# Six of layer 0's normalisations on GpSimd instead of VectorE, with new orders for the front

## The chip, the cores and the metric

The kernel runs on one core of one Trainium2 chip. The core has five engines that run side by side, each working through its own list of instructions in order: TensorE (PE in the profile; its weight loads are PEld), VectorE (DVE), ScalarE (ACT), GpSimd (POOL) and SyncE (SP), which here only starts DMAs. They wait for one another on semaphores. The metric is the device time of one execution in microseconds (us).

## The reference

A block of four layers works on x, 2048 tokens of 448 features, in bfloat16.

```
x = x + A(layernorm(x));  x = x + B(layernorm(x))     # layers 0 and 1
x = x + A(layernorm(x));  x = x + B(layernorm(x))     # layers 2 and 3

layernorm(x) = (x - mean) / sqrt(var + 1e-5)           # over the 448 features, no weights
A: qkv = x @ wqkv; 16 heads of 28; each token attends to 8 tokens,
   itself and those 2, 4, ... 14 before it; softmax; @ wo
B: (x @ w_gate) * (x @ w_up) @ w_down                  # 448 -> 1792 -> 448
```

## The kernel before

**Tiling.** Tokens lie on partitions in 16 blocks of 128 (even tokens first, then odd ones, so that a stride of 2 becomes a neighbour). Layer 0 projects its queries and keys in five chunks of 256, 512, 512, 512 and 256 tokens: chunk 0 is blocks 0 and 1, chunk 1 blocks 2 to 5, chunk 2 blocks 6 to 9, chunk 3 blocks 10 to 13, chunk 4 blocks 14 and 15. The attention works in groups of 120-token query tiles (group 0 has one, the others two).

**A block's way in layer 0** (`ln_chunk`): a DMA loads it into `x_sb`; VectorE takes its statistics (L584, `bn`) and combines them (L586, `mv`); ScalarE makes the inverse deviation with a logarithm and an exponential (L587, L589, `rstd`), for one, two or four blocks at a time; one instruction normalises (L605, `xn`), reading 2 x 256 features of `x_sb` (the two stretches overlap, so that 448 features become four rows of 128) and writing 512 bfloat16 values to one of five slots of `xn_sb`, block B to slot B modulo 5; TensorE transposes them into PSUM (L615, L619, `Tps`); ScalarE or VectorE evicts the transposed block into `xnTa` (L626, L629, `T`). Before, all sixteen `xn` of layer 0 are VectorE's.

**What follows.** TensorE projects queries and keys (`xnTa` with `WQK`) and values (`xnTa` with `WV`), both at L353. ScalarE or VectorE evicts them (L715 for queries and keys, L780 to L807 for values). VectorE masks the queries for two heads (L826, `Qz`), TensorE makes the scores (L838, `Sh`), ScalarE their exponentials (L848, `Ex`), VectorE the minimum with a mask `MK` (L855), TensorE the weighted values (L873, `Ah`); their copies and sums (L887, L891), the normalisation by the denominators (L901 to L914) and the output projection (`wo_g`, L353) end the layer. `WQK` is filled from a staging buffer by eight copies (L523, `wqk`), which the first projection waits for, and eight small ones (L531, `wqp`), which those from chunk 2 on wait for.

**What sets the order.** Nothing is decided on the chip. `build` creates the operations (`sc.add`) and numbers them as they come; each names the engines that may run it, its dependencies and a planned duration. `ORDER` holds, written out for each engine, the numbers in the order in which the engine runs them; an operation runs on the engine in whose list its number stands. `BANKS` gives each user of PSUM its banks of eight; an operation that takes a bank waits for the instruction that evicts the bank's last holder. `emit` turns all of it into instructions with semaphore waits. A wait stops the engine's whole list. TensorE starts with sixteen matmuls on a cleared buffer (`warm`, L515), among which the transposes of blocks 0 and 1 stand.

The planned durations (325.0 for an `xn`) are used by no instruction. `HEAD_P`, priorities and planned durations have no effect on the program once the orders are written out.

Of the kernel before, what the change touches and what calls it, by code (L numbers as in the profile page):

```python
# [5 lines left out]
ALU = mybir.AluOpType  # L6
# [91 lines left out]
def grp_nc(g):  # L98
# [36 lines left out]
    ),  # L135
    "dve": (
# [18 lines left out]
    ),  # L155
    "pool": (
        "24 18 28 29 25 39 40 32 33 35 41 26 20 22 21 30 27 36 19 31 34 42 37 43 44 68 66 38 77 23 76"
    ),
# [223 lines left out]
def build(nc, A_x, A_wqkv, A_wo, B_w_gate, B_w_up, B_w_down, out):  # L382
# [16 lines left out]
    mv = sb([128, NBLK, 2], dt.float32, "mv")  # L399
    lnv = sb([128, NBLK], dt.float32, "lnv")  # L400
    rstd = sb([128, NBLK], dt.float32, "rstd")
# [26 lines left out]
    sc = Sched()  # L428
# [9 lines left out]
    def one(fn, key=None):  # L438
        return [(fn, key)]
# [134 lines left out]
    def ln_chunk(li, j, prio):  # L574
        par = li % 2
# [552 lines left out]
```

## Time and profile before

| what | value |
|---|---|
| median of 3 runs | 380.56 us (380.43 to 381.18) |
| the profiled execution, its own time | 380.47 us |
| its span, first to last instruction | 378.7 us |
| TensorE busy | 373.6 us |
| VectorE busy | 285.4 us |
| ScalarE busy | 200.0 us |
| GpSimd busy | 7.8 us |
| granted TensorE clock, mean | 1.0 |

Times inside the execution count from the span's start. A busy TensorE is not one at its peak: the ends of its pipelined matmuls are modelled, and consecutive ones overlap in the rows, so its pace is read from start to start. A row of the timeline gives start, length, engine, line, operation, what it writes and reads, the shapes and the number of instructions merged; in brackets the engine's idle time before it and what ended it. A row of a group gives the number of instructions, then busy time in all and the mean of one in ns, then idle time before them. GpSimd's copies and mask building fill the first 11 us; after 22 us it does nothing.

### The profile page before, as it was taken

What the parts mean: (1) busy time and instruction counts of PE and PEld (TensorE: products, weight loads), DVE (VectorE), ACT (ScalarE), POOL (GpSimd) and SP (SyncE); (2) the same over time, 40 slices, a digit from 0 to 9 for tenths busy, and PEclk for the clock granted to TensorE, in tenths of its full rate; (3) what the DMA queues carried; (4) which work ended last, traced back from release to release, by engine and by line L of the source; (5) the groups of instructions that cost most, each with busy time, mean ns of one, the idle gap of its engine ahead of it and who ended that gap; (6) DMA issues with size and microseconds to landing.
All of it is one profiled execution on the core that took longest, in us unless ns stands there. A gap on an engine that the chain in (4) does not pass through costs nothing.

```text
span 378.7 us, 14371 instructions
## 1 busy us (share of the span) xinstructions
PE 373.6 (99%) x6376; PEld 208.7 (55%) x6376; DVE 285.4 (75%) x647; ACT 200.0 (53%) x384; POOL 7.8 (2%) x35
## 2 busy tenths in 40 slices
PE   8999999999999999999999999999999999999997
PEld 3645577644554445544676666645555444445764
DVE  7998999999867953878698598559699778446324
ACT  4897895778715355246548215638647533043310
POOL 6000000000000000000000000000000000000000
PEclk9999999999999999999999999999999999999999
DMA  7665544500250216312104123510106102312002
GB/s 260 167 163 144 112 113 95 81 10 13 31 86 5 58 28 93 43 28 50 25 10 64 27 29 63 93 31 5 29 12 102 35 5 54 74 42 70 2 2 85
DMA packets 56401, 23.10 MB, mean 61 GB/s; under 512 B 46004, under 2 KB 56324, under 8 KB 56340
## 3 DMA queue, kind: packets, MB, share of 16 engines
q1 hardware_dynamic: 56196, 22.14, 28.1%
q8 instruction: 50, 0.82, 0.9%
q14 instruction: 11, 0.09, 0.1%
q10 hardware_dynamic: 144, 0.06, 0.1%
HBM read 8.59 MB, written 2.71 MB: 30 GB/s over the span
## 4 chain that ended last, share of the span: by engine, by line
PE 96%; ACT 2%; POOL 1%; DVE 1%; issue 0%; DVEq 0%; POOLq 0%
PE ps L353 86%; PE ps L356 4%; PE ps L838 2%; PE ps L873 2%; PE ps L997 1%; POOL hT L493 1%; ACT E_sb L848 1%; PE ps L619 0%; PE ps L515 0%; ACT xnTa L626 0%; ACT qk L715 0%; DVE Qz L826 0%; PE ps L615 0%; ACT v_sb L807 0%; ACT xnTa L629 0%
## 5 line engine op out<-in xcount | busy, mean ns | idle before, releaser
L353 PE MATMUL ps<-xnTb,WGU 64*128 64x512 bf16 (+1 forms) x1898 | 173.3, 332 | 0.0
L353 PEld LDWEIGHTS ps<-xnTb,WGU 64*128 64x128 bf16 x1898 | 91.4, 94 | 71.2 <-DVE hT L985 0.6
L982 ACT ACTIVATE g_sb<-ps 128x512 bf16<-128x512 f32 (+1 forms) x140 | 68.9, 509 | 92.4 <-PE ps L353 88.4
L985 DVE TENSOR_TENSOR hT<-g_sb,ps 128x512 bf16<-128x512 bf16 (+1 forms) x140 | 77.4, 573 | 38.2 <-ACT g_sb L982 37.3
L353 PE MATMUL ps<-WD,hT 64*128 64x448 bf16 x786 | 80.8, 349 | 0.0
L353 PEld LDWEIGHTS ps<-WD,hT 64*128 64x128 bf16 x786 | 37.4, 94 | 32.4 <-DVE hT L985 0.2
L353 PE MATMUL ps<-xnTa,WQK 64*128 64x512 bf16 (+1 forms) x490 | 52.1, 352 | 0.0
L946 DVE TENSOR_TENSOR x_sb<-x_sb,ps 128x448 bf16<-128x448 bf16 x62 | 36.6, 611 | 16.4 <-PE ps L353 16.3
L848 ACT ACTIVATE E_sb<-ps,shift_sb 128x1024 bf16<-128x1024 f32 (+1 forms) x36 | 37.9, 1071 | 14.2 <-PE ps L838 13.8
L605 DVE TENSOR_SCALAR xn_sb<-x_sb,mv,rstd 128x896 bf16<-128x896 bf16 (+1 forms) x64 | 35.0, 568 | 6.6 <-ACT rstd L589 5.8
L584 DVE BATCH_NORM_STATS2 st<-x_sb 128x6 f32<-128x448 bf16 x64 | 38.5, 615 | 1.0 <-DMA x_sb<-in_A_x_dram 0.7
L353 PEld LDWEIGHTS ps<-xnTa,WQK 64*128 64x128 bf16 x490 | 23.1, 94 | 20.9 <-DVE WQK L523 0.3
L715 ACT ACTIVATE qk<-ps 128x1024 bf16<-128x1024 f32 (+1 forms) x28 | 25.4, 931 | 14.2 <-PE ps L353 12.0
L902 ACT ACTIVATE R_sb<-R_sb 128x480 f32<-128x480 f32 (+1 forms) x34 | 20.4, 603 | 13.7 <-DVE R_sb L901 13.6
L855 DVE TENSOR_TENSOR E_sb<-E_sb,MK 128x1024 bf16<-128x1024 bf16 (+1 forms) x36 | 23.4, 655 | 4.6 <-ACT E_sb L848 4.6
L914 DVE TENSOR_TENSOR oT<-O_sb,R_sb 128x480 bf16<-128x480 f32 (+5 forms) x38 | 22.2, 600 | 5.3 <-ACT R_sb L903 5.3
L353 PE MATMUL ps<-wo_g,oT 64*128 64x448 bf16 x228 | 25.6, 349 | 0.0
L353 PE MATMUL ps<-WV,xnTa 64*128 64x336 bf16 (+3 forms) x252 | 23.0, 304 | 0.6 <-DVE O_sb L891 0.2
L901 DVE STREAM_SHUFFLE R_sb<-O_sb 128x480 f32<-128x480 f32 (+1 forms) x34 | 23.2, 691 | 0.0
L826 DVE TENSOR_SCALAR Qz<-qk,qmask 128x960 bf16<-128x960 bf16 (+1 forms) x36 | 14.7, 451 | 7.5 <-ACT qk L715 6.5
L903 ACT ACTIVATE R_sb<-R_sb 128x480 f32<-128x480 f32 (+1 forms) x34 | 20.0, 602 | 0.4
L587 ACT ACTIVATE lnv<-mv,eps_sb 128x2 f32<-128x2 f32 (+2 forms) x31 | 8.9, 293 | 19.1 <-DVE mv L586 19.1
(63 smaller groups left out, 221.0 us busy)
## 6 DMA issues: line engine op xcount, KB each, us to landing
out_dram<-x_sb SPq DMA_DIRECT2D x15, 112.0 KB, 1.8
x_sb<-in_A_x_dram SPq DMA_DIRECT2D x3, 448.0 KB, 5.6
hT<-in_A_wqkv_dram SPq DMA_DIRECT2D x4, 224.0 KB, 4.6
WGU<-in_B_w_gate_dram SPq DMA_DIRECT2D x4, 224.0 KB, 3.7
WGU<-in_B_w_up_dram SPq DMA_DIRECT2D x4, 224.0 KB, 4.3
WD<-in_B_w_down_dram SPq DMA_DIRECT2D x2, 448.0 KB, 4.0
WGU<-in_B_w_gate_dram SPq DMA_DIRECT2D x2, 336.0 KB, 4.6
WGU<-in_B_w_up_dram SPq DMA_DIRECT2D x2, 336.0 KB, 4.6
```

The source lines that it names most:

```text
L353: return lambda E: E.matmul(out(), lhs(), rhs(), start=start, stop=stop)
L584: sc.add("dve", one(lambda E, B=B: E.bn_stats(st6[:, B, :], x_sb[:, B, :]), ("bn", li, B)), 525.0, deps=[("x", li - 1, B)] + ([("xn", li - ...
L605: sc.add("dve", one(lambda E, B=B, dst=dst, src=src: E.tensor_scalar(dst, src, mv[:, B, 0:1], rstd[:, B:B + 1], ALU.subtract, ALU.mult), ( ...
L715: return E.activation(dst, src, ACT.Copy) if hasattr(E, "activation") else E.tensor_copy(dst, src)
L848: return E.activation(E_sb[:, slot, 2 * hp:2 * hp + 2, 0:w], ps[:, b0:b0 + 2, 0:w], ACT.Exp, bias=shift_sb[:, 0:1], scale=SCALE)
L855: return E.tensor_tensor(e, e, MK[:, kind, 0:nc].unsqueeze(1).unsqueeze(1).to_broadcast([128, 2, w // nc, nc]), ALU.min)
L901: sc.add("dve", one(lambda E: E.stream_shuffle(R_sb[:, rs, 0:w], O_sb[:, os_, 0:w], [DH] * 32), ("Rs", li, qb)), dve_est(w) + 20.0, deps=[ ...
L902: sc.add("act", one(lambda E: E.activation(R_sb[:, rs, 0:w], R_sb[:, rs, 0:w], ACT.Ln), ("Rl", li, qb)), act_est(w, False), deps=[("Rs", l ...
L914: return E.tensor_tensor(oT[:, :, (a + 256) % HALF:(a + 256) % HALF + z - a], O[:, :, a - tok:z - tok], R_sb[:, rs, 0:w].rearrange("p (h n ...
L946: sc.add("dve", one(lambda E: E.tensor_tensor(x_sb[:, B, :], x_sb[:, B, :], ps[:, bk[w], 0:D], ALU.add), ("x", li, B)), dve_est(D), deps=[ ...
L982: sc.add("act", one(lambda E, gs=gs, bk=bk: E.activation(g_sb[:, gs, 0:nt], ps[:, bk[0], 0:nt], ACT.Copy), ("G", li, j, fc)), act_est(nt), ...
L985: sc.add("dve", one(lambda E, gs=gs, bk=bk, fc=fc: E.tensor_tensor(hT[:, fc, hs, 0:nt], g_sb[:, gs, 0:nt], ps[:, bk[1], 0:nt], ALU.mult), ...
```

## The change

The normalisation of layer 0's blocks from 6 on may now run on GpSimd too, and new lists are written out for all five engines up to about 50 us, with new banks (110 of 299 entries, most of them in the front). The tails of the lists of TensorE (274 of its 404 entries), ScalarE, VectorE and SyncE are unchanged. No operation is added or dropped. Decoded by number, the changes that the prediction speaks of are these.

- GpSimd's list gains `xn` of blocks 8, 7, 12, 11, 10 and 15 (numbers 154, 151, 176, 173, 170, 191); three `wqk` copies (65, 67, 69) and two `wqp` copies (78, 72), and gives one `wqp` copy (76) to VectorE. The identity for the transposes (18, 19) moves to its start, two of the three masks (31, 38) to near its end.
- VectorE's list clears `wo_g` (17) before the warm-up buffer (15), takes block 0 (100, 108) before block 1 (104, 111), and loses the six `xn`, the `wqk` copies 64, 69 and 70, the `T` of blocks 9, 12 and 15 (159, 178, 193) and two key copies of chunk 3 (511, 512). It gains the `T` of blocks 4, 6, 7 and 11 (134, 150, 153, 175), three key copies (202, 362, 598), two value copies (244, 245) and two output copies (220, 256).
- ScalarE's list takes what VectorE loses except the `xn` and 69, and gives what VectorE gains. The `wqk` copies 64 and 70 stand before the value copies 209, 240 and 241.
- TensorE's list moves, among others, block 0's transposes ahead of block 1's; 229 (second half of a projection of chunk 1) ahead of block 7's transposes; 217 and 218 between 247 and 248; 592 ahead of the output projection 266; 375 (values) ahead of the scores 381 and 382; 406 next to 405 and 388 next to 387; 533 away from 532.
- SyncE's list orders some stores to and transposes from the values' buffer in HBM (L724) anew.

```diff
@@ ORDER @@
     "pe": (
-        "47 48 49 50 51 52 53 54 55 112 56 57 58 59 109 60 61 62 206 130 127 207 238 133 136 239 198 194 232 195 233 196 200 199 197 201 228 226 155 149 227 229 "
-        "230 158 152 231 171 211 189 212 356 192 174 357 180 354 247 248 177 355 502 217 218 503 595 253 596 352 254 353 242 591 243 506 504 507 505 266 592 267 "
-        "371 271 272 372 358 508 359 509 593 277 278 381 382 375 594 376 405 589 406 590 387 310 307 388 313 319 322 304 290 316 291 328 340 532 533 334 325 331 "
+        "47 48 49 50 51 52 53 54 109 55 56 57 58 59 112 60 61 62 127 206 130 207 133 238 136 239 198 196 199 194 197 200 232 201 233 228 195 226 229 152 227 149 "
+        "230 158 155 231 171 189 211 212 180 356 192 177 174 357 354 247 217 218 248 355 502 595 253 503 352 254 353 596 506 504 507 505 242 591 243 592 266 267 "
+        "371 271 272 372 358 508 359 509 277 278 375 381 382 376 593 594 405 406 589 590 387 388 307 310 319 304 313 322 290 316 291 328 340 334 532 331 325 343 "
...
     "act": (
...
+        "14 102 103 110 106 107 118 119 113 124 125 131 208 64 70 209 240 241 204 205 146 147 203 237 168 169 235 186 234 187 159 236 213 214 178 193 249 250 "
...
     "dve": (
...
+        "17 15 45 100 101 16 104 108 116 105 117 114 115 120 111 121 126 122 123 129 128 132 135 140 63 134 137 138 162 142 141 143 160 139 144 145 184 166 182 "
+        "161 164 163 167 148 165 202 46 157 185 153 183 150 210 179 156 188 75 172 76 190 74 73 71 181 246 215 216 175 362 220 219 251 221 222 270 252 256 255 "
...
     "pool": (
-        "24 18 28 29 25 39 40 32 33 35 41 26 20 22 21 30 27 36 19 31 34 42 37 43 44 68 66 38 77 23 76"
+        "18 24 28 32 19 21 33 25 34 39 20 40 41 29 35 42 36 37 22 26 30 27 43 65 67 68 69 66 23 154 151 44 176 173 170 78 72 77 31 38 191"
     ),
...
@@ ln_chunk @@
-            sc.add("dve", one(lambda E, B=B, dst=dst, src=src: E.tensor_scalar(dst, src, mv[:, B, 0:1], rstd[:, B:B + 1], ALU.subtract, ALU.mult), ("xn", li, B)),
-                   325.0 if par == 0 else 540.0, deps=[("rstd", li, B), ("mv", li, B), ("x", li - 1, B), prev], prio=prio - 0.2)
+            sc.add(("dve", "pool") if li == 0 and B >= 6 else "dve", one(lambda E, B=B, dst=dst, src=src: E.tensor_scalar(dst, src, mv[:, B, 0:1], rstd[:, B:B + 1], ALU.subtract, ALU.mult), ("xn", li, B)),
+                   {"dve": 325.0, "pool": 800.0} if par == 0 else 540.0, deps=[("rstd", li, B), ("mv", li, B), ("x", li - 1, B), prev], prio=prio - 0.2)
```

Of the banks, the prediction speaks of those of the first projection (198, from 23 to 45, which the first value projection, 206, holds before it) and of the scores of groups 3 and 4 (381 and 382, from 01 and 67 to 67 and 45; 405 and 406, from 01 and 45 to 67 and 45).

79 rows, old and new, of tables (BANKS, ORDER) are left out of this document.

## The prediction

> **What bounds the kernel now.** I read the page first: the engines' shares and the shares of the chain of work that ended last.
>
> ```profile
> span 378.7 us, 14371 instructions
> PE 373.6 (99%) x6376; PEld 208.7 (55%) x6376; DVE 285.4 (75%) x647; ACT 200.0 (53%) x384; POOL 7.8 (2%) x35
> PE 96%; ACT 2%; POOL 1%; DVE 1%; issue 0%; DVEq 0%; POOLq 0%
> ```
>
> TensorE is busy for 99% of 378.7 us and holds 96% of the chain, and the change takes no matmul away. An edit gains only where TensorE waits; since it runs without a break afterwards, I take a shift made in the front to reach the end one for one. Next, the chain in order of time (start, length, what), for the places where it leaves TensorE.
>
> ```profile
> 9.27 0.59 ACT xnTa L629
> 21.47 0.34 DVE WQK L531 x2
> 21.81 0.30 DVE xnTa L629
> 39.43 2.12 ACT E_sb L848 x2
> 42.74 0.98 ACT qk L715
> 43.75 0.85 DVE Qz L826 x2
> 44.60 0.57 DVE O_sb L887
> ```
>
> Behind 9 us there are three: an eviction at 9.3; copies into the projection weights (L531) and an eviction of a transposed block (L629) at 21.5; and from 39.4 a path of exponentials, key copy, masked queries and output copy. TensorE's timeline gives their size.
>
> ```profile
> 9.91 0.74 PE L353 MATMUL ps<-WV,xnTa 64*128 64x448 bf16 x6 [0.22 <-ACT xnTa L629]
> 11.51 6.10 PE L353 MATMUL ps<-xnTa,WQK 64*128 64x256 bf16 x82
> 20.30 1.03 PE L353 MATMUL ps<-xnTa,WQK 64*128 64x512 bf16 x8
> 21.17 0.28 PE L619 MATMUL ps<-ident,xn_sb 64*128 64x64 bf16 x8
> 21.41 0.32 PE L838 MATMUL ps<-Qz,qk 64*64 64x144 bf16 x8
> 22.16 0.32 PE L838 MATMUL ps<-Qz,qk 64*64 64x144 bf16 x8 [0.21 <-DVE xnTa L629]
> 22.52 0.82 PE L353 MATMUL ps<-xnTa,WQK 64*128 64x512 bf16 x6
> 25.84 1.68 PE L353 MATMUL ps<-xnTa,WQK 64*128 64x512 bf16 x14
> 27.45 0.32 PE L873 MATMUL ps<-E_sb,v_sb 64*32 64x72 bf16 x32
> 44.74 0.64 PE L838 MATMUL ps<-Qz,qk 64*64 64x128 bf16 x32 [0.30 <-ACT qk L715]
> 45.63 0.60 PE L353 MATMUL ps<-WV,xnTa 64*128 64x336 bf16 x6 [0.24 <-DVE O_sb L891]
> ```
>
> Start to start, 20.30 to 21.17, four pairs of 512 columns take 0.87: 0.217 a pair. Seven from 25.84 should let the next start at 27.36; it started at 27.45. So a change of tile shape costs about 0.1, an excursion to attention matmuls and back 0.2. The marked idle (0.22, 0.21, 0.30, 0.24) with about as much again that overlapping matmuls hide makes roughly 1.3 us, estimated, 0.35% of the run: all that there is to win.
>
> **The change part by part.** Decoded by the numbering of the operations, the orders give GpSimd six normalisations, of blocks 8, 7, 12, 11, 10 and 15 in that order, two more than its short description says. Their durations, and those of their neighbours:
>
> ```profile
> L605 DVE TENSOR_SCALAR xn_sb<-x_sb,mv,rstd 128x512 bf16<-128x512 bf16 x16 | 6.2, 404 | 0.3 <-ACT rstd L589 0.3
> L523 POOL COPY WQK<-hT 128x448 bf16<-128x448 bf16 x2 | 1.1, 558 | 2.0 <-DMA hT<-in_A_wqkv_dram 2.0
> L531 POOL COPY WQK<-hT 128x64 bf16<-128x64 bf16 x1 | 0.2, 244 | 11.2 <-PE ps L619 11.2
> L497 POOL TENSOR_TENSOR MK<-hT 128x72 bf16<-128x72 bf16 x3 | 1.0, 330 | 0.1
> 20.00:25.00 5.00, 4.75 (x104) 2.50 (x98) 4.99 (x20) 4.66 (x7) 0.44 (x3) 1.00 0.77 185
> ```
>
> (1) Removed from VectorE: six of sixteen, 6.2/16 = 0.39 each, 2.3 us. Other moves (two key copies to ScalarE; three key copies, two value copies, two output copies back) nearly cancel this. VectorE at 4.99 of 5 in 20 to 25 us (third figure of the row) is relieved by little. These blocks are transposed by TensorE, so no DMA moves with them.
>
> (2) Price of one on GpSimd: no row shows it. Copies of 64 and 448 elements give (558 - 244)/384 = 0.82 ns an element, so 0.61 us for 512: the low end. The sum of two tensors, 330 for 72 elements, less the same fixed 0.19, is 1.9 ns: 1.18 us, the high end. One tensor is read, so I stand nearer the copy: 0.8. The GPSIMD Engine Reference of the Trainium skill (section 3.1) gives 1.8 cycles an element at 1.2 GHz for a tight loop, 769 ns measured there for 512; with a fixed 0.19 that would be 0.96, an estimate by that page, and the sum below 0.3 higher. No row here shows it.
>
> (3) Where that lies.
>
> ```profile
> 15.65 0.21 ACT L589 ACTIVATE rstd<-lnv 128x4 f32<-128x4 f32 x1
> ```
>
> The inverse deviation of blocks 6 to 9 was ready at 15.86; ScalarE now makes it behind two key copies of 256 columns, at 16.2 by my count. Blocks 8 and 7 then end at 17.0 and 17.85, before TensorE wants 7 at 18.4. The transposing buffer has five slots, so block 12 waits for the transposes of block 7, block 11 for those of block 6. In the new order I put these at 18.4 and 19.4 (TensorE has 0.85 more of projections ahead of block 7's transposes than it had before 17.4), so block 11 starts at 19.65 and block 10 ends at 19.65 + 2 x 0.8 = 21.2. TensorE wants it at 21.2, as before (21.17). No slack: each 0.1 on the price costs 0.2. Queued on GpSimd behind the wait: three weight copies (0.24 each, needed by the first projection of chunk 2), two mask sums (needed by the first attention minimum), block 15. These follow by 22.5 and 23.3, in time if block 10 is. At 0.61 the part costs nothing, at 1.18 it costs 0.8. Then VectorE's queue (masked queries, block 13, one eviction, block 14, the eviction of block 10) puts the second score matmul at 22.15 as before, and chunk 2's projection at 22.9 with one more transpose done: **+0.1**.
>
> (4) Two engines at one memory.
>
> ```profile
> 21.51 0.24 POOL L531 COPY WQK<-hT 128x64 bf16<-128x64 bf16 x1 [11.21 <-PE ps L619]
> 22.03 0.41 DVE L531 COPY WQK<-hT 128x64 bf16<-128x64 bf16 x4
> 20.00 1.13 DVE L605 TENSOR_SCALAR xn_sb<-x_sb,mv,rstd 128x512 bf16<-128x512 bf16 x3
> ```
>
> Four small VectorE copies take 0.41 alone, so two about 0.25; the two at 21.47, beside GpSimd's copy at 21.51, took 0.34. So VectorE stood still for 0.09 while GpSimd streamed 64 elements. With 512, a VectorE normalisation, masking or weight copy could stand for up to the whole 0.8. From 19.65 to 21.2 GpSimd works nearly without a break, and VectorE has there two maskings and block 13, all ahead of block 10's eviction. Full blocking makes that eviction end at 23.0 instead of 22.1: +0.9. None: 0. I take **+0.4**, since by my count VectorE's new queue stands idle twice for some 0.3 just before, waiting for transposes. "SBUF — State Buffer" in the Trainium skill (Who interferes with whom) states the full form: such operations exclude one another for the whole instruction. By it the sum would carry 0.9 here; the 0.09 agrees in kind and is too short to tell the size.
>
> (5) The start. The order clears wo_g ahead of the warm-up operand and starts with block 0.
>
> ```profile
> 0.93 0.27 DVE L476 MEMSET hT<- 128x256 uint32 x1 [0.93 <-PEq L1113]
> 1.34 0.81 DVE L476 MEMSET wo_g<- 128x896 uint32 x1
> 1.26 4.02 PE L515 MATMUL ps<-hT 128*128 128x512 bf16 x9 [1.26 <-DVE hT L476]
> 7.67 0.81 PE L515 MATMUL ps<-hT 128*128 128x512 bf16 x3
> 9.75 1.03 ACT L523 ACTIVATE WQK<-hT 128x448 bf16<-128x448 bf16 x2
> 11.65 0.36 ACT L789 ACTIVATE v_sb<-ps 128x224 bf16<-128x224 f32 x1
> ```
>
> The sixteen warm-up matmuls start 0.8 late, at 0.43 each (9 in 4.02) until TensorE speeds up; at 7.67 three need 0.81 with their tail. Block 0's eviction comes earlier and the wait at 9.91 goes. But ScalarE now makes its two weight copies (1.03) ahead of the value copies whose bank the first projection takes: I get 11.65 against 11.51, **+0.15**; 0 if the warm-up costs nothing, +0.5 if speed comes 0.8 later.
>
> (6) 36 to 51 us.
>
> ```profile
> 33.20 3.19 PE L353 MATMUL ps<-xnTa,WQK 64*128 64x512 bf16 x28
> 36.34 0.93 PE L353 MATMUL ps<-wo_g,oT 64*128 64x448 bf16 x8
> ```
>
> Fourteen pairs at 0.217 from 33.20 end at 36.24, so the output projection at 36.34 waited 0.1; a projection moved ahead of it fills that: **-0.1**. At 44 a value projection goes ahead of the scores that wait for masked queries, on another bank, so both waits shrink: 0.65 to about 0.15. Groups 3 and 4 keep their halves together: two excursions fewer, -0.4; the value projection now splits another, +0.1. Against it: both scores of group 4 now take the banks of group 3's scores, so the second waits for two exponentials.
>
> ```profile
> 45.21 2.12 ACT L848 ACTIVATE E_sb<-ps,shift_sb 128x1024 bf16<-128x1024 f32 x2
> ```
>
> With 2.12 for the pair, begun 0.2 later than here, they end at 47.5, and the score is due at 47.1: +0.4. Net **-0.4** (-0.8 to 0). Later group 5's two halves part: one excursion more, **+0.2**. SyncE's reordered stores and transposes cost nothing: they serve groups some 10 us later.
>
> Sum: 0.1 + 0.4 + 0.15 - 0.1 - 0.4 + 0.2 = +0.35. The profiled execution took 380.47 (span 378.7 and 1.8 around it), 0.1 under the median of 380.56. So 380.8.
>
> **The rivals.**
> Faster: the front's waits go and no new ones come. For it: GpSimd is used for 7.8 us of the span, and 1.3 us of waits are marked. Against: points 3 and 5. Parts 3 to 5 at their lower ends (0) and part 6 at -0.8 give 0.2 - 0.1 - 0.8 = -0.7; with the wait at 9.9 won as well, -0.9: 379.6.
> Slower: GpSimd becomes the bound of the transposes from block 10 on. It decides from the point where one normalisation takes over 0.8 or VectorE is blocked for all of it. Full blocking is 0.5 above my value: 381.3; with 1.0 us a piece, 0.4 more: 381.7. For it the 0.09; against it the gaps in VectorE's queue.
> Absorbed: the shift doesn't reach the end, because VectorE sets the pace further on. For it:
>
> ```profile
> 50.00:60.00 10.00, 10.00 (x219) 7.91 (x217) 10.00 (x27) 8.85 (x21) 0.00 (x0) 1.00 0.42 109
> ```
>
> VectorE is busy for all 10.00 us there. Against it: TensorE is too. It gives 380.5.
>
> **How the numbers follow.** A measurement of this kernel can tell about 0.2%, 0.76 us. The forecast, within 0.76 of 380.56, gets 0.40, and the absorbed case 0.10, also no change: 0.50. Slower by more: 0.26, by GpSimd. Faster by more: 0.24. The range goes from 379.6 (the faster case) to 381.7 (blocking and 1.0 us).
>
> **What would show it.** GpSimd's rows for xn_sb near 0.8 us (2); block 10's transposes on TensorE at 21.2 without idle ahead of them (3); VectorE's normalisations and maskings longer than 404 ns while GpSimd runs (4); the first projection at 11.65 (5); idle ahead of the scores near 47.5, and none ahead of the value projection near 45 (6). The forecast is wrong if GpSimd's operation is under 0.65 with no stretched neighbour, or if a wait for xn_sb on GpSimd appears before block 10 or 15.

## The result and the profile after

The changed kernel takes 391.75 us (median of four, 391.24 to 392.28) where the kernel before takes 380.87 beside it (380.43 to 381.85): ratio 1.0282, 95% interval 1.0256 to 1.0308. It is slower by 10.9 us. The profiled execution took 391.64 us. The page of the kernel after, its head and the row of the granted clock (40 slices of 9.7 us, in tenths):

```profile
span 389.6 us, 14369 instructions
PE 378.0 (97%) x6376; PEld 210.3 (54%) x6376; DVE 287.7 (74%) x643; ACT 198.5 (51%) x378; POOL 22.2 (6%) x45
PEclk9997999999999999999999999999999999999999
```

GpSimd's busy time rose by 14.4 us, and one slice, the fourth, has a clock below full. GpSimd's timeline in that stretch (start, length, what, how many; in brackets the idle time before):

```profile
16.66 4.14 POOL L605 TENSOR_SCALAR xn_sb<-x_sb,mv,rstd 128x512 bf16<-128x512 bf16 x2 [5.52 <-ACT rstd L589]
...
21.36 6.51 POOL L605 TENSOR_SCALAR xn_sb<-x_sb,mv,rstd 128x512 bf16<-128x512 bf16 x3 [0.41 <-PE ps L619]
27.82 0.56 POOL L531 COPY WQK<-hT 128x48 bf16<-128x48 bf16 x3
28.34 0.59 POOL L497 TENSOR_TENSOR MK<-hT 128x72 bf16<-128x72 bf16 x2
28.92 2.13 POOL L605 TENSOR_SCALAR xn_sb<-x_sb,mv,rstd 128x512 bf16<-128x512 bf16 x1
```

One normalisation takes 2.07 to 2.17 us here, not 0.8. TensorE's timeline shows what waits for it:

```profile
12.04 6.92 PE L353 MATMUL ps<-xnTa,WQK 64*128 64x256 bf16 x90
20.86 0.29 PE L619 MATMUL ps<-ident,xn_sb 64*128 64x64 bf16 x8 [1.90 <-POOL xn_sb L605]
...
27.92 0.61 PE L619 MATMUL ps<-ident,xn_sb 64*128 64x64 bf16 x16 [4.04 <-POOL xn_sb L605]
...
29.94 1.46 PE L353 MATMUL ps<-xnTa,WQK 64*128 64x512 bf16 x6 [0.32 <-DVE WQK L531]
...
49.50 0.93 PE L353 MATMUL ps<-WV,xnTa 64*128 64x448 bf16 x8
...
65.67 0.94 PE L353 MATMUL ps<-wo_g,oT 64*128 64x448 bf16 x8
```

The first projection starts at 12.04 (before: 11.51), block 7's transposes wait 1.90 and block 10's 4.04. Block 10's stand at 27.92 where they stood at 21.17: 6.75 of the loss is there by then. Two rows of the kernel before answer the last two; the first of them, a value projection behind group 2's scores, serves below as **the marker**:

```profile
39.53 0.93 PE L353 MATMUL ps<-WV,xnTa 64*128 64x448 bf16 x8
...
55.64 0.92 PE L353 MATMUL ps<-wo_g,oT 64*128 64x448 bf16 x8
```

The marker is 9.97 late, the later row 10.03, the end of the span 10.9. What comes between 6.75 and 9.97 falls into the time in which the clock was low. Four stretches of 3.41 us of the kernel after, with the busy time of TensorE first and the granted clock third from the end:

```profile
24.34:27.75 3.41, 0.00 (x0) 0.00 (x0) 0.39 (x2) 0.63 (x1) 3.41 (x2) 1.00 0.60 167
27.75:31.16 3.41, 2.92 (x46) 1.40 (x48) 2.80 (x9) 1.37 (x2) 3.30 (x7) 0.50 0.38 100
31.16:34.57 3.41, 3.41 (x40) 1.56 (x38) 2.06 (x5) 1.09 (x2) 0.00 (x0) 0.50 0.73 169
34.57:37.98 3.41, 3.41 (x122) 1.73 (x119) 2.74 (x8) 2.72 (x3) 0.00 (x0) 1.00 0.58 132
```

Behind a stretch without a matmul TensorE ran 6.8 us at half its clock, which can cost up to 3.4 (an estimate, half of 6.8). The Trainium skill, "TensorE: Matmul & The Clock Gate", Part 1, has a free-running window of 3413 ns, and an idle one throttles the array to half rate. The trace agrees: the clock changes at 27.75 and at 34.57, 6.82 or twice 3.41 apart, and falls to 0.50.

The loss in parts: start 0.5; the two waits for GpSimd 5.9 as marked, and 0.3 more that overlapping matmuls hide; slow clock and the wait for the weight copies at 29.94 together 3.2; behind 65 us 0.9. In what follows, a marker is good to about 0.2 us, since the start varies from run to run: the first projection starts at 11.23 to 11.70 in the profiles of the kernels with the old orders of the front, and at 11.91 to 12.42 in those with the new ones. The experiments ask three things. Why does one instruction take 2.1 us? Would the orders have paid with a cheaper one? Is the wait alone to blame, or the clock?

### The profile page after: what moved, and what is told of

Same layout as the page of the kernel before. It is cut to its first block, busy times and chain, and to the rows that moved or that the text cites. A ratio compares the mean times of both kernels' runs of the same rounds, so it can differ in the third digit from the quotient of the medians.

```text
span 389.6 us, 14369 instructions
## 1 busy us (share of the span) xinstructions
PE 378.0 (97%) x6376; PEld 210.3 (54%) x6376; DVE 287.7 (74%) x643; ACT 198.5 (51%) x378; POOL 22.2 (6%) x45
## 5 line engine op out<-in xcount | busy, mean ns | idle before, releaser
L353 PE MATMUL ps<-xnTa,WQK 64*128 64x512 bf16 (+1 forms) x490 | 54.0, 362 | 0.5 <-DVE WQK L531 0.3
L605 DVE TENSOR_SCALAR xn_sb<-x_sb,mv,rstd 128x896 bf16<-128x896 bf16 (+1 forms) x58 | 33.9, 605 | 6.9 <-ACT rstd L589 5.9
L587 ACT ACTIVATE lnv<-mv,eps_sb 128x2 f32<-128x2 f32 (+2 forms) x31 | 8.9, 292 | 20.7 <-DVE mv L586 18.4
```

What stands on the lines that cost most here:

```text
L353: return lambda E: E.matmul(out(), lhs(), rhs(), start=start, stop=stop)
L605: sc.add(("dve", "pool") if li == 0 and B >= 6 else "dve", one(lambda E, B=B, dst=dst, src=src: E.tensor_scalar(dst, src, mv[:, B, 0:1], r ...
```

## The experiments

All times of one table; "marker" is how much later than 39.53 the marker starts, "one" the length of one normalisation on GpSimd.

| kernel | one, us | marker | median, us | ratio to before (95%) |
|---|---|---|---|---|
| before | none there | 0 | 380.8 | 1 |
| after | 2.1 | +9.97 | 391.75 | 1.0256 to 1.0308 |
| after, all six back on VectorE | none there | +2.97 | 384.50 | 1.0078 to 1.0108 |
| after, only 12 and 11 on GpSimd | 2.08 | +3.25 | 384.33 | 1.0079 to 1.0110 |
| after, with fill matmuls | 2.1 | +8.28 | 390.09 | 1.0231 to 1.0267 |
| after, copies | 0.61 | +2.38 | 383.97 | 1.0068 to 1.0094 |
| after, sums | 1.04 | +5.10 | 387.13 | 1.0132 to 1.0170 |
| after, one operation | 1.57 | +6.26 | 388.73 | 1.0196 to 1.0224 |
| after, copies, three evictions back | 0.61 | +1.80 | 383.50 | 1.0057 to 1.0083 |
| before, six on GpSimd | 2.1 | +6.71 | 387.99 | 1.0168 to 1.0204 |
| before, only 10 on GpSimd | 2.12 | +0.79 | 381.41 | 1.0008 to 1.0027 |
| before, 11 and 12 on GpSimd | 2.3 | +0.07 | 381.22 | 1.0004 to 1.0026 |
| before, groups 3 and 4 reordered | none there | not comparable | 381.74 | 1.0015 to 1.0038 |

**The price by itself.** Ten GpSimd instructions are put into the last layer of the kernel before, where GpSimd has nothing else to do; they work on buffers that nobody reads any more.

```diff
+    E.tensor_scalar(two(pb), dup(pa[:, 0:448]), pc[:, 0:1], pc[:, 1:2], ALU.subtract, ALU.mult)   # as in the kernel, twice
+    E.tensor_scalar(pb, pa, pc[:, 0:1], pc[:, 1:2], ALU.subtract, ALU.mult)
+    E.tensor_scalar(pb[:, 0:256], pa[:, 0:256], pc[:, 0:1], pc[:, 1:2], ALU.subtract, ALU.mult)
+    E.tensor_scalar(pb, pa, pc[:, 0:1], None, ALU.mult)
+    E.tensor_scalar(pb, pa, 0.5, 0.5, ALU.subtract, ALU.mult)
+    E.tensor_copy(pb, pa)
+    E.tensor_tensor(pb, pa, pa, ALU.mult)
```

> The kernel before, with ten GpSimd instructions added during the last layer, where GpSimd is otherwise idle and nothing waits for them. Two of them repeat the moved normalisation in its exact form (overlapping source, two per-partition scalars), the others change one thing each: a plain source, half the length, one operation, immediate scalars, a copy, a product of two tensors. Theory G (the operation itself is that slow on GpSimd): the repeated form takes 2.0 to 2.2 us here too, as in the changed kernel's rows, and one of the other forms shows what makes it so; half the length should then take 1.1 to 1.2. Rival M (VectorE's work beside it makes it slow): it takes 0.6 to 1.2 here, where VectorE is less busy. The time of the kernel stays within 0.5 us of the one before.

Measured: 380.67 us (one run), and in GpSimd's timeline of this kernel

```profile
336.88 2.08 POOL L1075 TENSOR_SCALAR WQK<-WQK,R_sb 128x512 bf16<-128x512 bf16 x1
339.05 2.08 POOL L1076 TENSOR_SCALAR WQK<-WQK,R_sb 128x512 bf16<-128x512 bf16 x1
341.23 1.22 POOL L1077 TENSOR_SCALAR WQK<-WQK,R_sb 128x256 bf16<-128x256 bf16 x1
342.55 1.57 POOL L1078 TENSOR_SCALAR WQK<-WQK,R_sb 128x512 bf16<-128x512 bf16 x1
344.21 1.94 POOL L1079 TENSOR_SCALAR WQK<-WQK 128x512 bf16<-128x512 bf16 x1
346.21 0.61 POOL L1080 COPY WQK<-WQK 128x512 bf16<-128x512 bf16 x1
346.90 1.04 POOL L1081 TENSOR_TENSOR WQK<-WQK 128x512 bf16<-128x512 bf16 x1
```

The form of the kernel takes 2.08 far from the front's traffic too, so VectorE's work beside it isn't what makes it slow. The overlapping view costs nothing (2.08 with a plain one), scalars from memory 0.14, the second operation with its scalar 0.5. An element costs (2.08 - 1.22)/256 = 3.4 ns. The copy (0.61) and the product of two tensors (1.04) lie near the two bounds that the prediction took, 0.61 and 1.18. The operation itself lies outside them.

**The orders without the price.** The kernel after, with all six back in VectorE's list, near where they stood before.

```diff
-    pool, end of the list: 66 23 154 151 44 176 173 170 78 72 77 31 38 191
+    pool, end of the list: 66 23 44 78 72 77 31 38
+    dve: 151 ahead of 148, 154 behind 157, 170 176 behind 150, 173 behind 188, 191 behind 181
```

> The changed kernel with all six normalisations back on VectorE, everything else (orders, banks, the other moves) as changed. Theory G (the whole loss comes from GpSimd's normalisations): 380 to 381.2 us, and TensorE's waits ahead of the transposes of blocks 7 and 10 are gone, its clock at 1.0 throughout. Rival O (the new orders lose time by themselves: late warm-up, bank waits): over 382, with idle that is not ahead of those transposes.

Measured: 384.50. Theory G's expectation was missed by 3.3, and rival O's came: the new orders lose 3.7 with no normalisation on GpSimd at all. Between 16 and 28 us VectorE is busy for 11.83 of 12 us here and ScalarE for 8.87; the windows view gives 11.38 and 10.96 for the kernel before. So VectorE carries here both the six normalisations and the evictions that the change gave it; the kernel with copies, below, takes the normalisations off VectorE.

**A covered instruction.** The same, but blocks 12 and 11 stay on GpSimd, with the weight copies between them.

```diff
+    pool, end of the list: 66 23 44 31 38 176 78 72 77 173
```

> The changed kernel with only the normalisations of blocks 12 and 11 on GpSimd, the two that TensorE wants last, the other four back on VectorE; GpSimd's weight copies and mask sums ahead of block 11. Theory G: at 2.1 us each they end at about 21.0 and 23.7, about when TensorE wants them, so no wait over 0.5 us: 380.2 to 381.5. Rival (any normalisation on GpSimd costs its length): 2 us or more above the kernel with all six on VectorE.

Measured: 384.33, no different from the kernel above (384.50), and 2.8 above what was expected, for the same reason. GpSimd's timeline:

```profile
19.41 2.08 POOL L606 TENSOR_SCALAR xn_sb<-x_sb,mv,rstd 128x512 bf16<-128x512 bf16 x1 [7.04 <-DVE qk L716]
23.18 0.58 POOL L532 COPY WQK<-hT 128x48 bf16<-128x48 bf16 x3 [1.70 <-PE ps L620]
23.75 2.07 POOL L606 TENSOR_SCALAR xn_sb<-x_sb,mv,rstd 128x512 bf16<-128x512 bf16 x1
```

Both take 2.1 us and TensorE's waits do not name GpSimd: the medians show no cost of an instruction of that length where it is early enough. The trace shows a small one, on VectorE. Beside the first, two of VectorE's normalisations took 0.98 together, and 0.73 in the kernel above; beside the second, three small weight copies took 0.66 and not 0.33. The marker is 0.28 later than in the kernel above.

**The clock.** Eighteen matmuls on the cleared buffer stand ahead of block 10's transposes in the kernel after, so that TensorE works while it would wait.

```diff
+    sc.add("pe", 18 x matmul(ps[:, fb[0], :], warm[:, 0:128], warm), 3840.0, deps=["c_warm"], acquire=fb)   # 1670 ahead of 171
```

> The changed kernel with 18 matmuls on the cleared warm-up buffer ahead of block 10's transposes (into the bank that these take next), so that TensorE is not idle while it waits for GpSimd. Theory G with the clock as its second step (idle of 4.2 us halves the clock for 6.8 us, which costs about 3.2): the wait stays, the clock stays at 1.0, and the time falls by 2.5 to 3.3 us to 388.5 to 389.3. Rival: the stretch at half clock lies beside waits anyway: no change, within 0.5 us of 391.75.

Measured: 390.09, 1.66 less. TensorE's timeline (L1068 is the fill; 17 of its 18 matmuls are in the record):

```profile
24.00 3.83 PE L1068 MATMUL ps<-hT 128*128 128x512 bf16 x17 [0.16 <-issue]
27.82 0.41 PE L620 MATMUL ps<-ident,xn_sb 64*128 64x64 bf16 x16
...
29.83 0.82 PE L354 MATMUL ps<-xnTa,WQK 64*128 64x512 bf16 x6 [0.66 <-DVE WQK L532]
31.00 0.52 PE L620 MATMUL ps<-ident,xn_sb 64*128 64x64 bf16 x24 [0.35 <-POOL xn_sb L606]
```

The wait is as long as before (27.82), the granted clock is 1.000 throughout. So the halved clock is a consequence of the idle stretch, as expected, and it is worth less than the 2.5 to 3.3 expected: a TensorE at full pace runs into VectorE's last weight copies (0.66), which stand in its list behind block 10's eviction, and into block 15's normalisation (0.35), queued on GpSimd behind block 10.

**Price and response.** Three kernels put a cheaper instruction into the six places of the kernel after. They leave out part of the computation: the copies and the sums leave out subtraction and scaling for these six blocks, the third the subtraction.

```diff
-    E.tensor_scalar(dst, src, mv[:, B, 0:1], rstd[:, B:B + 1], ALU.subtract, ALU.mult)
+    E.tensor_copy(dst, src)                              # or
+    E.tensor_tensor(dst, src, src, ALU.add)              # or
+    E.tensor_scalar(dst, src, rstd[:, B:B + 1], None, ALU.mult)
```

> Kernel after, but the six normalisations on GpSimd are plain copies (0.61 us each in the probe, where the moved form took 2.08). This leaves out the subtraction of the mean and the scaling for these six blocks. Theory P (the price of one instruction on GpSimd is the cause, and the new orders are sound when it is low): chain from TensorE's transposes of block 7 at x: block 10 would be ready at x + 0.5 + 3 x 0.61 = x + 2.3, wanted at x + 2.9, so no wait for GpSimd remains; start late by 0.5; time 381 to 382. Rival O (the new orders lose by themselves, as the kernel with all six back on VectorE did with 384.5): 383.5 to 385 also here.

> Kernel after, but the six normalisations on GpSimd are a sum of the input with itself (1.04 us each in the probe); the subtraction of the mean and the scaling are left out for these blocks. Theory P: no wait at block 7 (16.66 + 2 x 1.04 = 18.7 against 18.8 wanted), at block 10 x + 0.5 + 3 x 1.04 - (x + 2.9) = 0.7 us of wait, TensorE's clock stays whole: 0.7 to 0.9 above the copy's kernel, 381.8 to 382.8. Rival O: the same time as the copy's kernel, 383.5 to 385.

> Kernel after, but the six normalisations on GpSimd have one operation in place of two (1.57 us each in the probe); the subtraction of the mean is left out for these blocks. Theory P: block 7 late by 16.66 + 2 x 1.57 - 18.8 = 1.0 us, block 10 by 0.5 + 3 x 1.57 - 2.9 = 2.3 us, both shorter than the wait that halved the clock: 3.3 us above the copy's kernel, 384.3 to 385.5, with the granted clock at 1.0. If the clock halves as in the kernel after (a wait of 4.2 us), 3 us more. From 0.61 to 2.08 us of price the time is then not a line: flat up to 0.8, about 5 us per us behind it, and a step of some 3 us between 1.57 and 2.08. Rival O: 384 to 386 with no wait for GpSimd above 1 us.

Measured: 383.97, 387.13 and 388.73, and 391.75 for the kernel after. The last two lie above what either theory gave. Theory P is right that the price sets the time: 7.8 us between 0.61 and 2.08. Rival O is right too about the base: the copies' kernel, which waits nowhere for GpSimd, is still 3.2 above before. Its waits of TensorE from 15 to 35 us:

```profile
PE ps L620 <- DVE xn_sb L606: 0.7, 1, 0.7
PE ps L354 <- DVE WQK L532: 0.4, 1, 0.4
PE ps L354 <- DVE xnTa L630: 0.4, 1, 0.4
```

Neither theory had the clock where it came. The kernel with sums waits 0.6 for GpSimd, as worked out, but its three waits lie together, and two stretches of it read

```profile
21.92:25.33 3.41, 1.63 (x44) 0.81 (x40) 3.41 (x8) 2.01 (x4) 3.13 (x7) 1.00 0.65 142
25.33:28.74 3.41, 3.02 (x36) 1.51 (x38) 2.58 (x10) 1.65 (x3) 0.00 (x0) 0.50 0.66 167
```

Behind a stretch in which TensorE was busy for 1.63 of 3.41 us the clock was halved for the next one, which costs up to 1.7 us. The executions of this kernel show the cost by themselves: three had a mean granted clock of 0.996 and took 387.03 to 387.24 us, the fourth had 1.000 and took 385.40. In the kernel with one operation the same comes behind a stretch of 0.91, on top of 3.3 us of waits for GpSimd. So the response has steps, and the first came with a price of 1.04, in three executions of four.

Busy time alone doesn't say when the clock goes. The kernel after waits 1.90 ahead of block 7; in the stretch with that wait, counted back from 27.75 in steps of 3.41, it is busy for less, and its clock stayed whole in the next (1.00 from 20.92 to 24.33). With six moved in the old orders (below) it was halved behind a busier one. The first row is of the kernel after, the second of the other:

```profile
17.51:20.92 3.41, 1.51 (x18) 0.55 (x16) 2.05 (x9) 1.93 (x4) 3.41 (x3) 1.00 0.54 128
```

```profile
21.71:25.12 3.41, 2.03 (x42) 0.90 (x40) 2.92 (x13) 2.98 (x5) 2.86 (x2) 1.00 0.67 153
```

The 1.51 are nearly all projections; the 2.03, and the 1.63 above, are for more than half transposes and scores, on smaller tiles. What the matmuls do may count beside how long they run; no run here tests it.

**Why the orders lose.** In the copies' kernel three evictions that the change moved from ScalarE to VectorE go back to ScalarE (202, 150, 362).

```diff
-    dve: 165 202 46, 153 183 150 210, 175 362 220
+    dve: 165 46, 153 183 210, 175 220
+    act: 202 behind 237, 150 behind 235, 362 behind 193
```

> The kernel with copies in place of the six normalisations (which leaves out the subtraction of the mean and the scaling there; 383.97 us), with three evictions that the change moved from ScalarE to VectorE back on ScalarE: the first scores' operand of group 0 (0.65 us), block 6's transposes (0.4) and one operand of group 2 (1.23). Theory V (the orders lose because VectorE was filled again with evictions; its waits ahead of TensorE at 19.8, 22.2, 23.9 and 27.6 were 0.56, 0.82, 0.57 and 0.26 us): 1.0 to 1.6 less, 382.4 to 383.0. Rival S (the orders lose by the start and by TensorE's own sequence): no change, 383.7 to 384.2.

Measured: 383.50, 0.47 less, under half of what theory V said, though VectorE was relieved by 1.9 us. The two intervals in the table overlap, so even the 0.47 is only just more than noise. Windows 16 to 28 us of the copies' kernel, and then of this one (busy time of TensorE, its weight loads, VectorE, ScalarE, GpSimd):

```profile
16.00:28.00 12.00, 10.43 (x230) 5.62 (x230) 11.34 (x38) 9.08 (x18) 4.84 (x12) 1.00 0.57 141
```

```profile
16.00:28.00 12.00, 11.25 (x238) 5.87 (x236) 9.42 (x36) 11.18 (x21) 4.92 (x12) 1.00 0.58 136
```

Six normalisations had gone from VectorE, and its load was 11.34 against 11.38 before: the change filled it again with evictions. Taken off, the waits pass to others: the weight copies keep 0.4, block 14's normalisation 0.2, and 0.2 now goes to a key copy on ScalarE. VectorE's load is at most a part of the orders' loss; the larger part stayed, and what in the orders makes it isn't settled.

**The moves in the old orders.** The kernel before, with nothing else changed: first blocks 11 and 12, then block 10 alone, then all six in the sequence in which they are wanted.

```diff
-    pool, end of the list: 66 38 77 23 76
+    pool, end of the list: 66 38 23 173 77 76 176               # blocks 11 and 12; dve loses 173 176
+    pool, end of the list: 66 38 23 170 77 76                   # block 10; dve loses 170
+    pool, end of the list: 66 38 23 154 151 170 191 173 176     # six; dve loses them and takes 77 76 behind 78
```

> Kernel before with nothing changed but two normalisations, those of blocks 11 and 12, on GpSimd (2.08 us each). Theory P (an instruction on GpSimd costs what it is late, no more): block 11 runs 20.0 to 22.1, wanted at 23.3; the two copies for the packed weights behind it end at 22.5, as late as VectorE's own last copy; block 12 ends at 24.6, wanted at 25.7. Nothing is late, and VectorE, 0.4 us ahead from 20.7 on, shortens its wait at 21.8 (0.37 us) and perhaps the one at 22.3 (0.21): 380.1 to 380.8, ratio 0.9985 to 1.000. Rival C (an instruction on GpSimd costs by contention even where it is covered): 381.2 or more.

> Kernel before with nothing changed but one normalisation, that of block 10, on GpSimd: it runs 20.0 to 22.1 and is wanted by TensorE at 21.2, so it is 0.9 us late, where the two of the kernel with blocks 11 and 12 are not. Theory P: TensorE waits 0.9 us ahead of block 10's transposes, the wait of 0.37 us behind it goes, and the packed weights' copies on GpSimd end at 22.5: 0.5 to 0.9 above before, 381.2 to 381.7. Rival: no change, since VectorE gains what GpSimd loses: 380.5 to 380.9.

> The six normalisations on GpSimd (2.08 us each) in the orders of the kernel before, without the new search: GpSimd takes them as they are wanted (blocks 8, 7, 10, 15, 11, 12), the two copies for the packed weights go to VectorE. By the rows of before: block 8 ends at 18.0 where 17.4 is wanted (+0.55), 7 in time, 10 at 22.15 (+0.45 more), 15 at 24.5 (+0.35), 11 at 26.6 (+2.0), 12 in time: 3.3 us of waits for GpSimd, from which up to 0.7 of VectorE's waits come off, and 1.7 come on if the wait of 2 us halves the clock for one stretch of 3.4 us: 383.4 to 385.5. That would leave some 6 us of the changed kernel's loss to the new orders, above all to GpSimd's own, which takes blocks 12 and 11 ahead of 10. Rival (the new orders are fitted to slow instructions and the six cost that much in any order): 389 or more.

Measured: 381.22, 381.41 and 387.99. With 11 and 12 moved, GpSimd's timeline is

```profile
19.84 2.26 POOL L606 TENSOR_SCALAR xn_sb<-x_sb,mv,rstd 128x512 bf16<-128x512 bf16 x1 [9.31 <-ACT rstd L590]
22.06 0.39 POOL L532 COPY WQK<-hT 128x64 bf16<-128x64 bf16 x2
22.43 2.31 POOL L606 TENSOR_SCALAR xn_sb<-x_sb,mv,rstd 128x512 bf16<-128x512 bf16 x1
```

and the marker is 0.07 late, though the first projection started 0.17 early, at 11.34: 0.24 is lost in the front. Nothing is gained, since VectorE's two normalisations beside GpSimd's took nearly as long as the three that stood there before (1.13, in the prediction's part 4):

```profile
19.83 1.10 DVE L606 TENSOR_SCALAR xn_sb<-x_sb,mv,rstd 128x512 bf16<-128x512 bf16 x2
```

The median is 0.4 above before, at the lower end of what rival C gave (381.2 or more) and a little outside theory P's range. In the profiled execution the 0.4 come at 75 us, where TensorE waits for a transposing DMA of layer 1 and its next group starts 0.47 late:

```profile
PE ps L354 <- DMA xnTb<-xn_sb: 0.2, 1, 0.2
```

The kernel with block 10 moved has it too (0.3), the one with all six 1.3 of it; the profiles of before and after have none. Why this DMA lands later when normalisations move in the old orders isn't shown. So contention costs about what the move saves, and whether the rest is rival C's or this DMA's own isn't settled. With block 10 moved TensorE's timeline has

```profile
22.03 0.29 PE L620 MATMUL ps<-ident,xn_sb 64*128 64x64 bf16 x8 [0.91 <-POOL xn_sb L606]
```

0.9 us late, as worked out (21.2 wanted, 22.1 done), and the marker is 0.79 late. By the medians the two kernels can't be told apart; at the marker they can, in one profile each, and there an instruction costs about its lateness. With all six, the waits are

```profile
18.38 0.41 PE L620 MATMUL ps<-ident,xn_sb 64*128 64x64 bf16 x16 [0.69 <-POOL xn_sb L606]
...
23.12 0.29 PE L620 MATMUL ps<-ident,xn_sb 64*128 64x64 bf16 x8 [0.86 <-POOL xn_sb L606]
...
28.25 0.39 PE L620 MATMUL ps<-ident,xn_sb 64*128 64x64 bf16 x8 [2.03 <-POOL xn_sb L606]
```

where 0.55, 0.45 and 2.0 were expected. But the clock is halved for two stretches of 3.4 us and not one, and from 25.12 on, ahead of the wait of 2.03; the DMA's wait comes on top in the profiled execution, and the expectation (383.4 to 385.5) was 2.5 short. The rival's 389 isn't reached either: the same six moves in the old sequence cost 7.2, and the new orders 3.8 on top, not 6.

**A place behind the front.** The kernel before with TensorE's groups around 45 us in another sequence, which was to end the waits marked there (0.30 and 0.24).

```diff
-    pe: 593 277 278 381 382 375 594 376 405 589 406 590
+    pe: 277 278 375 381 382 593 376 594 405 589 406 590      # banks changed to match
```

> Kernel before with only the order of TensorE's groups around 44 to 46 us changed: the projection of the values goes ahead of the scores, and four halves of eviction pairs stand in another order and other banks. Theory: the waits of about 0.65 us there end, 380.0 to 380.5 (ratio 0.998 to 0.9995). Rival: the wait only moves to the next group, ratio 0.9995 to 1.003.

Measured: 381.74, ratio 1.0026 (1.0015 to 1.0038): slightly slower. TensorE's timeline:

```profile
47.11 0.42 PE L839 MATMUL ps<-Qz,qk 64*64 64x128 bf16 x16
48.45 0.50 PE L354 MATMUL ps<-xnTa,WQK 64*128 64x256 bf16 x6 [0.92 <-DVE v_sb L808]
```

The two waits went, and a wait of 0.92 for a value copy on VectorE came 3 us later. The rival (the wait moves on) was right.

## Why the prediction was wrong

**Step (2), the price, failed, and with it the sum.** It was bounded by a copy (0.61) and by a sum of two tensors (1.18), "one tensor is read, so I stand nearer the copy: 0.8". The probe shows 2.08, outside the bounds: the rows were of other operations, and the kind of operation decides, not the number of tensors read. The estimate taken there from the Trainium skill, "GPSIMD Engine Reference", section 3.1 (0.96), is less than half of what was measured. Of the 10.9 us, 7.8 go with the price, the clock included: that is what the kernel with copies is faster by.

**Step (3) had the mechanism, its slope was too small.** It saw no slack at block 10 and put each 0.1 of price at 0.2 us. With 2.08 that makes 2.6 us; the two marked waits make 5.9. Block 7 becomes late as well (20.80 by GpSimd's rows, against the 18.4 of the prediction and 18.96 in the trace), and behind its transposes, which free a slot, three normalisations follow before block 10 is done, so from there on the slope is three. The slower rival was this mechanism with the right place ("the transposes from block 10 on") and the right condition (over 0.8), priced for 1.0 at most.

**A term was missing: the clock.** Up to 3.2 us of the 10.9 came while TensorE ran at half rate behind the wait; the fill matmuls won 1.66 of it back, and in the kernel with sums one halved stretch cost 1.6 to 1.8. The before profile shows a whole clock, so no row pointed to it; the start's slow matmuls (0.43 each in step 5) were the only sign.

**Step (4)** took +0.4 for two engines at one memory, with full exclusion as the upper end. Three rows of VectorE's timeline of the kernel after; beside the first GpSimd makes weight copies, beside the other two its first two normalisations (16.66 to 20.80):

```profile
8.81 0.67 DVE L605 TENSOR_SCALAR xn_sb<-x_sb,mv,rstd 128x512 bf16<-128x512 bf16 x1
...
17.41 0.38 DVE L605 TENSOR_SCALAR xn_sb<-x_sb,mv,rstd 128x512 bf16<-128x512 bf16 x1
...
18.80 0.84 DVE L605 TENSOR_SCALAR xn_sb<-x_sb,mv,rstd 128x512 bf16<-128x512 bf16 x1
```

The one at 17.41 takes 0.38, less than the mean of 0.404 before, inside a GpSimd instruction of 2.1; that at 18.80 is stretched by 0.44, that at 8.81 by 0.27. So in these rows VectorE is delayed at times, by 0.44 at most, and not for a whole instruction of 2 us. The full form of the rule in the Trainium skill, "SBUF — State Buffer" (Who interferes with whom), isn't borne out by them. On the path are three small weight copies, beside block 15's normalisation:

```profile
29.22 0.66 DVE L531 COPY WQK<-hT 128x48 bf16<-128x48 bf16 x3
```

They took 0.33 in the kernel with all six back on VectorE, and the projection at 29.94 waits for them. That is near the step's +0.4; it was not what decided.

**Step (5)**: 12.04 against the 11.65 forecast, +0.5 and not +0.15, at the upper end that the step named. **Step (6)**: -0.4 and +0.2 were expected behind the marker; the two marked waits of before are gone, yet from the marker (+9.97) to the row at 65.67 (+10.03) nothing was won. **Step (1)** was right that VectorE is relieved by little, and drew no price from it. **The steps on the orders failed too, by 3.2 us.** With the instruction at 0.61 us, below the price forecast, they put the time at no change, and the copies' kernel is 3.2 slower: a price as low as forecast would not have saved the sum. The clearest miss is at the end of step (3), which counted VectorE's queue and put chunk 2's first projection at 22.9. In the copies' kernel, where TensorE waits nowhere for GpSimd, it starts 1.6 later, behind three waits that name VectorE:

```profile
24.46 0.82 PE L354 MATMUL ps<-xnTa,WQK 64*128 64x512 bf16 x6 [0.41 <-DVE WQK L532]
```

Of the 1.6, 0.3 is the start (11.95, where 11.65 was forecast). Another 0.9 comes between the marker and the end of the span. Some 0.3 of that 0.9 isn't the new orders': it comes where the kernel before is at 292 us, and TensorE waits there for a DMA in kernels with the old orders of the front too (0.20 with block 10 moved, 0.36 with groups 3 and 4 reordered).

The forecast named in advance what would refute it, "a wait for xn_sb on GpSimd appears before block 10 or 15", and that is the row at 27.92.

## What to carry to other kernels

The price of an operation that no row shows isn't bounded by other operations of the same engine: leave the upper end open, or measure it alone where the engine is idle, before an order is built on it. A longer instruction costs little while its cover holds, apart from what it slows on the engine beside it, and its whole lateness from there on, times the instructions queued one behind the other. Waits that empty much of some 3.4 us can cost TensorE its clock for the next 3.4 too. And test new orders apart from the price that they were made for: these lost 3.2 us even with an instruction that was cheaper than forecast.

## What the runs showed of the hardware

On GpSimd an operation with scalars on 128 x 512 bfloat16 took 2.08 us with two operations, 1.57 with one and 1.94 with constants, the product of two tensors 1.04 and a copy 0.61: the operation that reads two tensors is half as dear as the one that reads one. A normalisation on GpSimd, 2.08 us alone, took up to 2.31 beside VectorE's work, and three small VectorE copies took 0.66 beside one and 0.33 alone. TensorE's clock halved behind stretches of 3.41 us with 0, 0.91, 1.63 and 2.03 us of matmuls, and stayed whole behind ones with 1.51 and 2.95: no threshold in busy time fits all six. It stayed halved for one such stretch in the kernels with sums and with one operation, and for two in the kernel after and the one with six moved in the old orders; TensorE was busy for 2.92 us of the first of the two in the kernel after, and for 2.93 of the single one with one operation. What decides between one and two stays open.
